# One kernel's table of order rewritten: linear attention followed by a maxout feed-forward layer

## The chip, the cores and the metric

One core of one Trainium2 chip. The metric is the device time of one execution in microseconds (us). The core has five engines that run side by side: TensorE (PE in the profile; its weight loads are shown as PEld), VectorE (DVE), ScalarE (ACT), GpSimd (POOL) and SyncE (SP, which here only issues transfers). Each works through its own list of instructions in order; semaphores make one wait for another. Transfers (DMA) can be issued by SP, ACT and POOL.

## The reference

Eight batches of eight heads, 576 tokens of 64 channels; then 4608 tokens of 512 channels through a layer of 768.

```python
def phi(x):
    proj = np.einsum('bhsd,df->bhsf', x, w_phi)
    proj = proj - np.max(np.abs(proj), axis=-1, keepdims=True)
    return np.concatenate([np.exp(proj), np.exp(-proj)], axis=-1)
q_p, k_p = (phi(q), phi(k))
kv = np.einsum('bhsf,bhsd->bhfd', k_p, v)
z = np.sum(k_p, axis=2)
num = np.einsum('bhsf,bhfd->bhsd', q_p, kv)
den = np.einsum('bhsf,bhf->bhs', q_p, z)[..., None] + 1e-06
x = num / den                      # then to 4608 x 512, heads side by side
h = np.maximum(np.maximum(x @ w1, x @ w2), x @ w3)
out = h @ w_out
```

## The kernel before

**Attention.** The work is cut into 16 units of four heads. A unit loads q, k and v (`L`, `Lv`), brings q and k to bfloat16 (`C`, or in the transfer itself), turns them so that channels lie on partitions (`T` and its copy `Tc` through TensorE in the first four units, a transposing DMA later), projects them (`G`, line 531), takes the largest absolute value of each row (`r`, line 550, DVE), and the two exponentials of the k side (`ek`, line 544, ACT). The q side is projected again with its maximum subtracted (`M`, line 610 or 612/615) and exponentiated (`eq`, line 623, ACT). v is scaled by the exponential of k's maxima (`E`, line 581, ACT; `va`, line 585; `vd`, line 595, the 18-column cast beside it). `K` (line 639) makes the kv sums, `kv` (line 644) copies them out, `N` (line 657) multiplies with the q side, `x` (lines 663 and 664, DVE) divides. `X` turns the result back: through TensorE and a copy `Xc` (line 680) in the first two units, by a transposing DMA (line 687) later.

**Feed-forward.** Nine chunks of 512 tokens, one for each batch and one for the leftover tokens. The maximum of three products is rewritten: w2 and w3 have w1 subtracted (`wd`, line 781), so that h = x w1 + max(0, x(w2-w1), x(w3-w1)), and w1 is folded into w_out once (`wt`, `wm`, `mo`, lines 793 to 811, with `mo` the copy of the folded weight). Each chunk is 12 groups `up`/`up2` of four 128x512 matmuls (line 710), each evacuated by `t1` (line 718 on ACT or 720 on DVE) or `h` (line 716, DVE), then `down` (lines 738 and 743), a copy `osb` (line 751) and a `store` (line 758).

**Order.** The function builds 1471 nodes, numbered as they are made. Each node is one step with its instructions. `PLAN` is a table written out in the file, one word for each node: `51D0@14.7` is node 51, on DVE, buffer slot 0 where the node is the first to use a buffer, with the time 14.7 that a planner gave it. Letters: T is TensorE, D DVE, A ACT, G GpSimd, S SP. The program is issued in the order of the words, so each engine's list is that order restricted to its letter. The times are a planner's due times; on the chip nothing waits for them. They are used in one place: `fill` looks at the gaps between TensorE's due times and puts idlers into them, matmuls on a constant operand whose result nobody reads (line 838), down to gaps of 0.35 us before the due time 28.0 and 0.5 after, and only once the node that clears their operand (node 2) is due to have ended.

```python
n.eng, n.start = {"T": "PE", "D": "DVE", "A": "ACT", "G": "POOL", "S": "SP"}[what[at]], float(start)
n.end = n.start + n.costs[n.eng] + LATENCY[n.eng]
...
gap, t = n.start - free, max(free + 0.1, ready)
while gap > (0.35 if t < WARM else 0.5) and t < n.start - (0.3 if t < 10 else 0.2):
```

**Nodes that the texts name.**

| nodes | what they do |
|---|---|
| 0, 1; 2, 3 | constants: identity and its negative (GpSimd); the idlers' operand and zeros (DVE) |
| 8, 6; 12, 10 | the transfers of the two halves of q and of k of unit 0 (SP) |
| 9, 7; 13, 11 | their casts to bfloat16 (line 448) |
| 84 | the gate: a copy of one row of q (line 460) that holds GpSimd's loads until the first half of q is there |
| 85, 86; 157, 158 | loads of q, k of units 1 and 2 by GpSimd (line 457) |
| 1073, 1074, 1075, 1076 | loads of w1, w2, w3, w_out (line 416) |
| 87, 159 | loads of v of units 1 and 2 |
| 225, 226; 358, 359; 293 | loads of q, k of unit 3; of unit 5; of q of unit 4 |
| 17, 15, 19 | the transposes of unit 0 (line 488) |
| 47, 48, 51, 52; 49, 53 | `va` and `vd` of unit 0; 120, 121, 124, 125 and 122, 126 those of unit 1 |
| 1090, 1092, 1094, 1096 | `mo`, copies of the folded weight (line 811) |
| 81, 83; 154, 156 | `Xc` of units 0 and 1 |
| 229, 231, 233 | `Tc` of unit 3 (line 494) |
| 1099 | the first `up` group |
| 1466, 1470 | the last two stores |

Of the kernel before, what the change touches and what calls it, by code (L numbers as in the profile page):

```python
# [105 lines left out]
66T6@21.4 69T54@21.8 118D@21.8 68A@21.8 67A@22.1 107D@22.1 116A@22.4 163D@22.7 109T60@22.9 71A0@23.1 113D@23.3 100A@23.3  # L106
181T34@23.5 70A@23.8 112D@23.9 123A1@24.1 182A0@24.3 1091T5@24.3 165D@24.5 117D@24.7 119A@24.8 101A@25.0 185D0@25.1
111A@25.4 184D0@25.6 176T61@25.8 127T2@26.1 177A@26.2 179D@26.2 76T7@26.6 183A0@26.7 1092D@26.8 78T3@26.9 120G1@27.0
178A@27.2 136T6@27.2 77D00@27.4 129A1@27.7 133T4@27.7 79D1@28.1 125G@28.1 72T5@28.1 110A@28.1 74T7@28.4 135A@28.6
73D0@28.7 139T0@28.8 126A@29.1 1093T3@29.1 121G@29.2 138A@29.2 75D1@29.3 122A@29.7 140A@29.8 180D@30.0 137A@30.0  # L110
124G@30.3 130T5@30.4 134A@30.5 1094D@30.6 171T71@30.9 141A@31.0 166T64@31.2 128A@31.3 174D@31.4 1075G@31.4 142T30@31.5
172A@31.7 169D@32.0 1078G@32.2 131A@32.2 175D@32.6 186T27@32.6 143A1@32.8 1095T6@32.9 132A@33.1 189D@33.2 170D@33.5
188A@33.6 173A@33.8 145T3@34.1 1079G@34.2 144A@34.3 1096D@34.3 82T2@34.5 149T5@34.7 83A@34.9 146D10@34.9 80T1@35.1
151T0@35.3 168A@35.5 190D@35.6 1089T6@35.7 150D1@35.9 194A0@36.0 187A@36.2 361G1@36.3 81A@36.5 152D0@36.5 147T2@36.9
1090D@37.2 191T3@37.3 228T7@37.4 1077G@37.4 192A0@37.5 167A@37.7 148D1@37.8 193S@37.8 230T5@37.9 229D0@38.4 153T1@38.6
155T0@38.9 231D@39.0 154A@39.1 232T3@39.2 362G@39.5 239T64@39.6 233D@39.6 156A@39.6 249T27@39.8 242D1@40.0 234T51@40.0
# [5 lines left out]
379T24@48.0 367D0@48.2 203A@48.2 198T1@48.3 1121T0@48.5 365A0@48.7 214D@48.8 297G2@49.0 383D0@49.1 202A@49.2 1113T6@49.4
200A@49.6 1122D@49.7 199A@50.1 554S0@50.2 210T7@50.3 382D@50.3 207T5@50.4 1117T0@50.6 211A@50.6 296G@50.6 209A@50.9
1114D@50.9 380A@51.3 266T1@51.5 368D@51.5 1111T2@51.7 298S2@51.8 212A@51.8 381A0@52.1 1118D@52.1 427G0@52.5 1119T6@52.5
267A1@52.6 1112D@52.7 208A@53.0 1115T7@53.4 262A1@53.5 1120D@53.6 268A@53.7 263G1@54.1 265A@54.2 366A@54.3 374T40@54.4
1116D@54.5 369T25@54.6 423S1@54.7 384T61@54.8 371A@55.0 269T3@55.0 372D@55.1 360S0@55.2 1127T7@55.2 385A@55.5 387D@55.6
295S1@55.7 271A@55.7 377D@56.0 216T2@56.1 264G@56.2 553S0@56.2 270A@56.2 222T6@56.4 378D@56.6 370A@56.7 220T4@56.7
275T3@57.0 217D00@57.2 1128T@57.3 375A@57.3 376A@57.8 388D@57.8 373D@58.1 386A@58.2 389T2@58.6 281T01@58.7 221D1@58.7
392A0@58.9 276A@59.1 223D0@59.4 277A@59.5 314T54@59.8 282D1@60.0 272T6@60.1 315A1@60.2 390D0@60.3 1123T3@60.4 426G@60.4
317D1@60.5 391S@60.6 1129A0@60.7 283D@61.1 274A@61.2 278T0@61.2 318D1@61.4 304T25@61.4 557G1@61.5 428S0@61.6 280A@61.6  # L130
309T71@61.6 279A@61.9 1124T@62.0 307D@62.0 316A1@62.2 393G0@62.6 308D@62.6 273A@62.7 312D@63.2 218T0@63.3 305A@63.3
# [738 lines left out]
```

## Time and profile before

| | |
|---|---|
| runs | 291.5, 291.47, 284.21 us; median 291.47 |
| profiled execution | 284.58 us, its span (first to last instruction) 282.8 us |
| busy | TensorE 269.3, DVE 213.0, ACT 190.4, GpSimd 121.9 us |
| idlers | 14 matmuls, 5.6 us busy |
| transfers | HBM read 34.64 MB, written 9.44 MB |

A timeline row reads: start in us, length in us, engine, line of the kernel, operation, output<-inputs, shape, count, and in brackets the idle time of the engine before it with what ended it. A row of a group of instructions has the count, then busy us, mean ns of one, and the idle time before them. A row of waits reads: engine, tile and line, "<-" who released it: us in total, times, longest. A row of windows has for each engine the busy us and the instructions in that stretch, then the granted TensorE clock, the busy share of the DMA engines and GB/s. A group of DMA issues ends with the median us from issue to landing.

### The profile page before, as it was taken

The numbers are of one execution on the slowest core, as the hardware profiler recorded it, in microseconds if no ns is written. First come the engines' busy times: TensorE is split into PE (matmuls) and PEld (weight loads), VectorE is DVE, ScalarE is ACT, GpSimd is POOL, SyncE is SP. The second block draws the span as 40 slices with busy tenths as digits, with TensorE's granted clock in tenths as the row PEclk, the third lists the DMA queues.
The fourth block names the chain that finished last, engine by engine and source line by source line (L and its number), as shares of the span: only waits on it lengthen the run. The fifth ranks groups of instructions, "written<-read, shape, count | busy, mean of one in ns | idle before, by whom it ended". The sixth has DMA issues, their size and how long they took to land.

```text
span 282.8 us, 8452 instructions
## 1 busy us (share of the span) xinstructions
PE 269.3 (95%) x3497; PEld 152.7 (54%) x3536; DVE 213.0 (75%) x444; ACT 190.4 (67%) x445; POOL 121.9 (43%) x103
## 2 busy tenths in 40 slices
PE   3998999999999999999999999999999999999995
PEld 1565675466565555555565556654544555444443
DVE  4899999999889789888898879895683367036432
ACT  2789989997889999776895989758546750211010
POOL 4773999487458232808536755050535000000000
PEclk9999999999999999999999999999999999999999
DMA  6999959999998989996999997888143114500164
GB/s 214 219 211 286 295 91 233 273 313 199 276 216 293 197 166 288 307 234 168 252 246 198 304 199 194 165 172 208 70 93 68 41 41 93 111 2 0 39 139 157
DMA packets 67680, 51.43 MB, mean 182 GB/s; under 512 B 48762, under 2 KB 52922, under 8 KB 67642
## 3 DMA queue, kind: packets, MB, share of 16 engines
q1 hardware_dynamic: 62554, 42.87, 63.5%
q0 software_dynamic: 4576, 7.28, 12.2%
q10 hardware_dynamic: 512, 0.75, 0.7%
q8 instruction: 27, 0.44, 0.6%
q14 instruction: 11, 0.09, 0.1%
HBM read 34.64 MB, written 9.44 MB: 156 GB/s over the span
## 4 chain that ended last, share of the span: by engine, by line
PE 89%; DVE 7%; issue 1%; DMA 1%; ACT 0%; DVEq 0%
PE ups L710 33%; PE ops L743 16%; PE ops L738 10%; PE psn L657 7%; PE kvps L639 6%; PE psq L531 5%; PE psm L610 5%; DVE mqp L550 2%; PE pm L807 1%; DVE mk L550 1%; PE idler L838 1%; DMA q_raw<-in_q_dram 1%; DVE x_sb L664 1%; PE psm L612 1%; DVE w_bf L781 1%
## 5 line engine op out<-in xcount | busy, mean ns | idle before, releaser
L710 PE MATMUL ups<-xT,w_bf 128*128 128x512 bf16 x413 | 101.6, 379 | 1.1
L585 POOL TENSOR_TENSOR vab<-v_raw,em 128x1152 bf16<-128x1152 f32 (+1 forms) x35 | 66.8, 1926 | 60.8 <-ACT em L581 49.7
L544 ACT ACTIVATE Ek<-psk 128x512 bf16<-128x512 f32 (+1 forms) x156 | 82.7, 579 | 13.0 <-PE psk L531 10.0
L623 ACT ACTIVATE Eq<-psm 128x512 bf16<-128x512 f32 (+1 forms) x160 | 82.2, 588 | 12.6 <-PE psm L610 11.9
L710 PEld LDWEIGHTS <-w_bf 128*128 128x128 bf16 x432 | 40.2, 98 | 45.3 <-issue 0.7
L550 DVE TENSOR_REDUCE mqp<-psq 128x4 bf16<-128x512 f32 (+1 forms) x80 | 48.8, 632 | 4.0 <-PE psk L531 3.4
L743 PE MATMUL ops<-wout_bf,hT 128*128 128x512 bf16 (+2 forms) x216 | 50.3, 373 | 0.5 <-issue 0.3
L550 DVE TENSOR_REDUCE mk<-psk 128x4 f32<-128x512 f32 (+1 forms) x78 | 48.4, 635 | 2.8 <-PE psk L531 1.5
L716 DVE TENSOR_TENSOR hT<-hT,ups 128x512 bf16<-128x512 bf16 x54 | 35.8, 681 | 12.8 <-PE ups L710 8.8
L751 ACT COPY osb<-ops 128x512 f32<-128x512 f32 x19 | 11.5, 606 | 34.3 <-PE ops L743 34.0
L664 DVE TENSOR_TENSOR x_sb<-psn,rden 128x320 bf16<-128x320 f32 x64 | 31.5, 492 | 2.4 <-DVE rden L663 0.2
L743 PEld LDWEIGHTS <-hT 128*128 128x128 bf16 x222 | 20.6, 98 | 22.3
L720 DVE TENSOR_SCALAR hT<-ups 128x512 bf16<-128x512 f32 x28 | 18.8, 686 | 17.3 <-PE ups L710 15.0
L657 PEld LDWEIGHTS <-Eq 128*128 128x128 bf16 x640 | 25.4, 97 | 8.3
L657 PE MATMUL psn<-kv_sb,Eq 128*128 128x65 bf16 x640 | 27.2, 194 | 0.1
L531 PE MATMUL psq<-w,qkT 64*128 64x128 bf16 x284 | 23.8, 217 | 0.4 <-DVE qkT L494 0.4
L738 PE MATMUL ops<-xT 128*128 128x512 bf16 x89 | 23.9, 379 | 0.3
L531 PE MATMUL psk<-w,qkT 64*128 64x128 bf16 x284 | 23.9, 217 | 0.0
L718 ACT ACTIVATE hT<-ups 128x512 bf16<-128x512 f32 x26 | 15.8, 616 | 11.8 <-PE ups L710 11.7
L610 PE MATMUL psm<-qkT,wphi_m 128*128 128x512 bf16 (+1 forms) x70 | 22.4, 358 | 0.6 <-DVE hT L720 0.5
L531 PEld LDWEIGHTS <-qkT 64*128 64x128 bf16 x568 | 16.4, 94 | 11.3 <-issue 8.2
L639 PE MATMUL kvps<-vab,Ek 64*128 64x65 bf16 x1152 | 20.5, 190 | 0.6 <-issue 0.6
(79 smaller groups left out, 233.3 us busy)
## 6 DMA issues: line engine op xcount, KB each, us to landing
out_dram<-osb SPq DMA_DIRECT2D x64, 128.0 KB, 2.7
v_raw<-in_v_dram SPq DMA_DIRECT2D x14, 576.0 KB, 6.1
k_raw<-in_k_dram SPq DMA_DIRECT2D x11, 576.0 KB, 4.9
q_raw<-in_q_dram SPq DMA_DIRECT2D x11, 576.0 KB, 5.2
w_bf<-in_moe_w_dram POOLq DMA_DIRECT2D x3, 768.0 KB, 9.0
v_raw<-in_v_dram POOLq DMA_DIRECT2D x2, 576.0 KB, 14.9
qk_bf<-in_q_dram POOLq DMA_DIRECT2D x3, 288.0 KB, 9.5
qk_bf<-in_k_dram POOLq DMA_DIRECT2D x3, 288.0 KB, 11.8
```

The source lines that it names most:

```text
L531: nc.tensor.matmul(ps()[:, i, :], lhsT=cols[r, :], rhs=w2[r, c, :], start=True, stop=True)
L544: nc.scalar.activation(Ek[s]()[:, tiles_of(t0, n), :], of(1), EXP, scale=1.0 - 2.0 * s)
L550: nc.vector.tensor_reduce((mq, mk)[c]()[:, tiles_of(t0, n)], of(c), AXX, ALU.max, apply_absolute_value=True)
L585: (nc.vector if n_.eng == "DVE" else nc.gpsimd).tensor_tensor(vab()[:, g, t0:t1, 0:D], vb()[:, t0:t1, :], em()[:, g, t0:t1].unsqueeze(2).t ...
L610: nc.tensor.matmul(psm()[:, 0:w], lhsT=wphi_m, rhs=rhs, start=True, stop=True)
L623: nc.scalar.activation(Eqb()[s][:, cols], psm()[:, 0:w], EXP, scale=1.0 - 2.0 * s)
L639: nc.tensor.matmul(kvps[ab]()[:, t // NT, g, :], lhsT=Ek[g]()[r, t, :], rhs=vab()[r, g, t, :], start=(t + g == 0), stop=(t == UT - 1 and g ...
L657: nc.tensor.matmul(psn()[:, c, :], lhsT=Eqb()[g][:, t0:t0 + P], rhs=kv()[:, pr, ab, g, :], start=(g == 0), stop=(g == 1))
L710: nc.tensor.matmul(ups(), lhsT=w_bf[i + 1][:, ct, j * P:(j + 1) * P], rhs=tokens_of(ct), start=(ct == 0), stop=(ct == CT - 1))
L716: nc.vector.tensor_tensor(hT()[:, j, :], hT()[:, j, :], ups(), ALU.max)
L738: nc.tensor.matmul(ops_()[:, 0:width], lhsT=tile_of(ct, tt), rhs=line_w[c_i > MOVE][:, ct, cols], start=(ct == 0), stop=False)
L743: nc.tensor.matmul(ops_()[:, 0:width], lhsT=hT()[:, j, tt * P:(tt + 1) * P], rhs=wout_bf[:, j, cols], start=False, stop=(j == JT - 1))
```

## The change

The table `PLAN` is replaced by another one; no other line is touched. It has the same 1471 nodes. 84 nodes stand on another engine (among them 24 `t1`, 14 `osb`, 14 `kv`, 14 `vd`, 6 `mT`, 2 `mo`), the order on every engine differs, and buffer slots (PSUM banks among them) are given out anew. On DVE 352 nodes stand in place of 370, on ACT 443 in place of 430, on GpSimd 107 in place of 98, on SP 110 in place of 114; TensorE keeps its 459. Between TensorE's nodes on 64 rows or 64 columns and the others there are 75 changes in place of 77. The last due time is 275.8 in place of 277.4; by the rules of `fill` the new due times make 20 idlers in place of 14, twelve of them (in place of four) ahead of the first transposes.

The start of both tables:

```diff
-4A@0.7 8S0@0.7 12S0@1.1 10S@1.6 6S@2.0 14S0@2.5 9D0@3.5 84G1@3.5 0G@3.7 2D0@4.1 85G@4.3 3D@4.3 13A@5.0 86G@5.0 5D@5.5
-1G@5.8 17T1@5.8 11D@5.9 1073G@6.3 18D0@6.6 7A@6.8 157G2@7.1 36T23@7.4 15T4@7.7 158G@7.8 38A0@7.8 39D0@7.8 31T56@8.3
-16D@8.4 1076G@8.5 32A0@8.8 34D@9.0 21T71@9.2 33A@9.2 87G1@9.3 26T24@9.4 25D0@9.6 37A@9.7 19T5@9.7 1074G@10.0 27A@10.2
-20D@10.2 24D@10.4 41T5@10.6 28A@10.7 358G1@10.8 29D@11.0 43A@11.1 23A@11.4 225G0@11.5 44D@11.6 30D@11.9 60T7@12.1
-40D@12.5 63T2@12.5 92T4@13.1 45D@13.1 64A0@13.2 88T3@13.3 35D@13.4 22A@13.7 89D1@14.0 46A0@14.1 54T6@14.2 50A@14.3
-42A@14.6 57T1@14.6 51D0@14.7 61A@14.8 94T35@15.2 65A@15.3 97D1@15.6 59A@15.8 226G@15.9 90T2@16.0 98D1@16.2 47G@16.6
-1085T3@16.6 93D@16.8 95A1@16.9 91D@17.0 1087T4@17.2 96A1@17.4 1086D0@17.6 52G@17.7 114T2@17.8 49A@17.9 62A@18.0
-1083T5@18.1 1088D@18.2 55A@18.5 99T37@18.7 1084D@18.8 359G1@18.8 58A@18.9 104T04@19.0 108D@19.4 115A@19.4 53G@19.5
-48G@19.7 160T5@19.9 102D@20.0 106A@20.1 164T1@20.4 56A@20.6 161D2@20.6 162T3@20.7 159G2@20.8 105A@21.1 103D@21.2
...
-124G@30.3 130T5@30.4 134A@30.5 1094D@30.6 171T71@30.9 141A@31.0 166T64@31.2 128A@31.3 174D@31.4 1075G@31.4 142T30@31.5
...
-294S0@43.5 238D@43.8 255A@43.9 293S0@44.0 245A@44.1 253D@44.4 204T4@44.4 1105T1@44.6 1104A@44.6 197G@44.7 1082G@44.9
...
+0G@0.7 2D0@0.7 4A@0.7 8S0@0.7 3D@0.8 12S0@1.1 1G@1.3 10S@1.6 6S@2.0 14S0@2.5 9D0@3.6 84G1@3.6 85G@4.1 5D@4.2 86G@4.8
+13A@5.1 1073G@5.5 11A@5.9 17T1@5.9 158G2@6.3 18D0@6.6 157G@7.0 7A@7.0 31T23@7.3 1076G@7.7 33A0@7.8 34D0@7.8 15T4@7.8
+32A0@8.2 36T56@8.4 16D@8.5 87G1@8.5 19T7@8.8 38A@8.8 20D@9.1 1074G@9.2 21T12@9.2 39D@9.3 26T47@9.5 23A@9.7 29D@9.9
+41T5@10.0 28A@10.1 25D0@10.5 42A@10.6 27A@10.9 44D@11.1 22A@11.4 24D@11.4 88T4@11.7 43A@11.8 30D@12.0 63T2@12.4
+89D1@12.6 60T1@12.8 65A0@13.0 35D@13.2 57T7@13.3 62A@13.5 45D@13.8 92T4@13.8 61A@14.0 40D@14.1 94T35@14.3 46A0@14.5
+90T1@14.7 95A1@14.7 97D1@14.7 47G0@14.8 64A@15.2 93D@15.3 54T3@15.5 98D1@15.5 50A@15.7 59A@15.9 49G@15.9 1085T4@15.9
+48G@16.1 91D@16.1 96A1@16.4 1083T2@16.4 1086D0@16.7 37A@16.8 1087T1@16.9 51G@17.2 53A@17.3 1084D@17.3 58A@17.4
+114T5@17.4 99T04@17.8 55A@17.9 118D@17.9 104T67@18.1 52G@18.3 56A@18.4 108D@18.5 162T2@18.7 103D@19.1 105A@19.2
+160T3@19.2 225G0@19.4 106A@19.7 107D@19.7 359G1@20.1 101A@20.2 102D@20.3 69T76@20.5 116A@20.7 358G1@20.8 161D2@20.9
+100A@20.9 115A@21.4 1088D@21.5 226G@21.5 109T04@21.6 119A1@21.7 71A0@21.9 164T3@21.9 117D@22.1 70A@22.1 66T1@22.3
+159G2@22.3 113D@22.4 1091T6@22.6 67A@22.7 68A@23.0 1075G@23.0 163D@23.0 123A@23.2 110A@23.4 112D@23.6 111A@23.9
+181T75@23.9 176T12@24.2 165D@24.2 183A0@24.4 1092D@24.4 139T0@24.5 121G1@24.5 136T3@24.8 182A0@24.9 179D0@25.0
+127T4@25.3 177A@25.3 185D0@25.6 124G@25.6 72T6@25.7 129A1@25.9 133T1@26.0 184D@26.2 140A@26.4 76T5@26.5 141A@26.6
+126G@26.7 73D00@26.8 120G@26.9 137A@26.9 78T7@27.0 74T0@27.3 134A@27.4 180D@27.4 1093T6@27.6 138A@27.9 125G@28.0
+77D1@28.0 128A@28.3 75D0@28.7 135A@28.8 130T3@28.9 293G0@29.1 178A@29.3 1094D@29.3 171T54@29.4 166T01@29.7 131A@29.8
```

and their ends:

```diff
-1459T2@269.7 1405A3@269.9 1406S@270.6 1456T@270.6 1460T@271.9 1457A0@272.1 1458S@272.7 1463T7@273.2 1461A1@273.4
-1452T@273.8 1462A@274.0 1464T@275.1 1453D2@275.3 1454A@276.1 1467T4@276.1 1465D3@276.3 1468T@276.6 1466A@276.9
-1469D0@277.1 1470S@277.4
...
+1457A1@271.0 1458A@271.6 1452T@272.1 1461D0@272.3 1462S@273.0 1464T@273.4 1453A3@273.6 1454A@274.2 1467T2@274.4
+1465D2@274.6 1468T@274.9 1466A@275.2 1469D1@275.4 1470A@275.8
```

More of the change, by code (lines that the diff above doesn't have):

```diff
@@ L112 @@
[L112 to L116, printed above, removed]
@@ L122 @@
[L122 to L126, printed above, removed]
@@ L127 @@
[L127 to L131, printed above, removed]
@@ new lines @@
+1027D@210.5 983A@211.0 1022D@211.1 1020A@211.5 1348D@211.7 1349T5@211.7 1026A@211.9 1023D@212.3 1359T7@212.6 1028D@212.9
+1341T3@213.4 1042A1@213.6 1360D@213.6 1021A@213.8 1044G1@214.0 993T6@214.3 1039T2@214.4 990T7@214.5 995A@214.6
+1040D1@214.7 1357T1@214.7 992A@214.9 1041S@214.9 1343T2@215.6 1043G@216.0 1332T@216.4 1344D@216.6 1358D@217.2
+1375T2@217.7 1333A2@217.9 1425G@218.1 1342A@218.4 1045G@218.4 996T10@218.7 1350A@218.9 994A@219.3 991A@219.6
+1061T35@219.8 998D0@220.0 997A@220.1 1351T6@221.0 1062A1@221.1 1063D@221.1 1325A1@221.3 984T7@221.8 1326S@221.9
@@ new lines @@
+1071D0@230.3 1064T1@230.6 1376T@230.9 1065D1@231.1 1072S@231.8 1367T3@232.2 1364T@233.1 1368T@234.4 1426G@235.4
+1372T@235.7 1369D1@235.8 1379T7@236.9 1383T6@237.8 1380A0@238.0 1377A3@238.5 1391T0@238.7 1384D@238.9 1378S@239.1
+1435T1@239.5 1392D@239.7 1334S@240.3 1431T3@240.4 1411T7@241.3 1381T2@242.1 1365A3@242.2 1432A1@242.6 1366S@242.8
+1437T6@243.0 1436A@243.1 1403T0@243.8 1370S@244.0 1438A@244.0 1382A@244.5 1397T5@244.7 1389T3@245.6 1395T1@246.4
+1385T6@247.3 1396D@247.5 1399T2@248.2 1386D@248.4 1387T1@249.0 1398D@249.1 1401T6@249.9 1388A@250.1 1390A@250.6
@@ new lines @@
+1400D@250.7 1407T5@250.8 1402D@251.3 1415T1@251.6 1393T3@252.5 1433T2@253.3 1394D@253.5 1373D2@254.1 1463T6@254.2
+1434D@254.7 1445T3@254.9 1374S@254.9 1408T@255.7 1446D@255.9 1427T4@257.0 1409A3@257.2 1447T2@257.9 1428D@258.1
+1443T3@258.7 1448D@258.9 1416T@259.6 1404T@260.9 1417D1@261.1 1449T5@262.2 1405A2@262.4 1406S@263.0 1429T4@263.1
+1439T2@263.9 1430D@264.1 1418S@264.2 1444D@264.7 1459T1@264.8 1440D@265.3 1294S@265.4 1451T0@265.6 1450D@265.9
+1455T4@266.5 1410S@266.6 1441T3@267.4 1412T@268.2 1442D@268.4 1456T@269.5 1413A2@269.7 1414S@270.3 1460T@270.8
```

227 lines of the change are left out of this document (112 added, 115 removed).

## The prediction

> **What bounds the kernel now.** I read the page's first part first, then the windows, then who waits for whom, and last the timeline of the first 42 us.
>
> ```profile
> span 282.8 us, 8452 instructions
> PE 269.3 (95%) x3497; PEld 152.7 (54%) x3536; DVE 213.0 (75%) x444; ACT 190.4 (67%) x445; POOL 121.9 (43%) x103
> ...
> core 0: us, PE busy (x) PEld busy (x) DVE busy (x) ACT busy (x) POOL busy (x), PEclk, DMA share, GB/s
> ...
> 10.00:40.00 30.00, 27.05 (x557) 19.42 (x561) 28.65 (x62) 26.46 (x69) 22.19 (x22) 1.00 1.07 232
> ...
> 40.00:280.00 240.00, 236.92 (x2904) 130.69 (x2935) 179.20 (x367) 160.42 (x372) 93.42 (x68) 1.00 0.74 175
> ```
>
> There are two stages. From 10 to 40 us VectorE (DVE) is busy 28.65 of 30 us, with ScalarE (ACT) close behind at 26.46: there the vector work is the bound. From 40 to 280 us TensorE is busy 236.92 of 240 and DVE only 179.20. What TensorE waits for in that second stage is this list of waits, for the window 40 to 280 and the matmuls alone, complete, and the first row of the same list for the weight loads:
>
> ```profile
> PE psm L610 <- DVE hT L720: 0.5, 1, 0.5
> PE ops L743 <- issue: 0.3, 2, 0.2
> ...
> PEld L531 <- issue: 8.2, 20, 0.4
> ```
>
> The matmuls lose 0.8 us in 240 to waits. So the second stage can hardly be shortened by any order of the same matmuls; what a new order can win must be won before 42 us, and TensorE then carries it to the end.
>
> The start and the end of the first stage, from the timelines of DVE, TensorE and ACT:
>
> ```profile
> 3.73 0.75 DVE L448 CAST qk_bf<-q_raw 128x576 bf16<-128x576 f32 x1 [3.73 <-DMA q_raw<-in_q_dram]
> 4.46 0.17 DVE L409 MEMSET idle<- 128x128 bf16 x1
> ...
> 7.46 0.69 DVE L494 COPY qkT<-tps 128x1024 bf16<-128x1024 bf16 x1 [0.29 <-PE tps L488]
> ...
> 4.68 1.89 PE L838 MATMUL idler<-idle 128*128 128x512 bf16 x4 [4.68 <-DVE idle L409]
> 6.37 1.05 PE L488 MATMUL tps<-ident,qk_bf 128*128 128x128 bf16 x8
> ...
> 8.70 0.62 PE L488 MATMUL tps<-ident,qk_bf 128*128 128x128 bf16 x8
> ...
> 5.64 0.67 ACT L448 CAST qk_bf<-k_raw 128x576 bf16<-128x576 f32 x1 [3.05 <-DMA k_raw<-in_k_dram]
> 7.42 0.67 ACT L448 CAST qk_bf<-q_raw 128x576 bf16<-128x576 f32 x1 [1.10 <-DMA q_raw<-in_q_dram]
> ...
> 40.63 1.18 ACT L680 COPY xT<-pxT 128x576 bf16<-128x576 bf16 x2 [0.77 <-PE pxT L677]
> ...
> 41.89 0.82 PE L710 MATMUL ups<-xT,w_bf 128*128 128x512 bf16 x2
> ```
>
> The idlers, which warm TensorE, start at 4.68 because DVE clears their operand behind a cast that waits for the first landing. The first eight transposes take 1.05 us, the same eight at 8.70 take 0.62: the first group ran at the slow clock.
>
> **The change, part by part.** (a) *Warm-up.* Nodes 2 and 3 go ahead of the first cast, so DVE clears the operand in the 3.7 us in which it waits anyway; by the rules of fill the idlers become 20 instead of 14, twelve of them before the first transposes. The transposes still start at 6.37, since they hang on the ACT cast of 5.64. They run warm: 1.05 - 0.62 = **-0.43 us**, straight on the chain (DVE waits for them at 7.46). Bounds: 0 if the clock is still slow at 6.37, -0.43 if not; I take -0.43.
>
> [...]
>
> (b) *Work taken from DVE.* Up to the first `up` group (node 1099) TensorE's nodes are the same ones in both tables. Before the transposes' copies of unit 3 DVE has four instructions fewer: a cast of k (11), one scaling of v (51) and two copies of the folded weight (1096, 1090).
>
> ```profile
> 10.01 0.68 DVE L550 TENSOR_REDUCE mqp<-psq 128x4 bf16<-128x512 f32 x1
> 10.61 0.68 DVE L550 TENSOR_REDUCE mk<-psk 128x4 f32<-128x512 f32 x1
> ...
> 15.65 0.75 DVE L585 TENSOR_TENSOR vab<-v_raw,em 128x576 bf16<-128x576 f32 x1
> ...
> L811 DVE CAST xT<-pm 128x512 bf16<-128x512 f32 x4 | 2.7, 684 | 0.4 <-PE pm L807 0.4
> ...
> 40.00 1.48 DVE L494 COPY qkT<-tps 128x1024 bf16<-128x1024 bf16 x3
> ```
>
> Two 0.68 us instructions follow each other at 0.60 (10.01, 10.61), so a removed one is worth 0.60 and the scaling about 0.70: 0.70 + 2 x 0.60 = **-1.9 us** of DVE's 28.65. The cast of k lies before 7.46, where DVE waits anyhow: 0.
>
> (c) *Given back at the end of the stage.* Node 156, the second copy of xT of unit 1, goes from ACT to DVE and stands behind the three copies of 1.48 us. Before, DVE's last division ended at about 40.08 and the ACT copies at 40.63 + 1.18 = 41.81, 1.73 later. After, it is about 1.40 for the three copies (0.08 of them overlapped) and 0.68 (the 684 ns of L811) for the copy: 2.08. **+0.3 us.**
>
> (d) *What ACT takes on.* Two folded-weight copies and one 18-column cast come, three 18-column casts go to GpSimd or away:
>
> ```profile
> L751 ACT COPY osb<-ops 128x512 f32<-128x512 f32 x19 | 11.5, 606 | 34.3 <-PE ops L743 34.0
> ...
> L595 ACT CAST vab<-em 128x18 bf16<-128x18 f32 x3 | 0.9, 302 | 0.0
> ```
>
> 2 x 0.606 + 0.302 - 3 x 0.302 = +0.61 us, so 26.46 becomes 27.07 in a stage that (a) to (c) shorten by 2.0 to 28.0. That is 97% busy, and ACT has 3.54 us of idle time in the stage today. Between nothing given back and all 2.0, I take **+0.4 us**: ACT only has to fill idle time that in part waits for DVE.
>
> (e) *GpSimd's queue.* The constants 0 and 1 move ahead of the gate, so the weights and the loads of units 1 and 2 are issued about 0.5 us sooner or a little more, beside the first q and k. Six loads (nodes 225, 359, 358, 226, 159, 1075) then stand in a row, behind five pieces of unit 0's v and ahead of unit 1's v.
>
> ```profile
> 12.35 0.71 POOL L457 DMA_DIRECT2D qk_bf<-in_q_dram  x1 [0.47 <-ACT Ek L544]
> 15.86 0.70 POOL L457 DMA_DIRECT2D qk_bf<-in_k_dram  x1 [2.80 <-DMA w_bf<-in_moe_w_dram]
> ...
> 20.80 0.76 POOL L470 DMA_DIRECT2D v_raw<-in_v_dram  x1
> ...
> 26.06 4.48 POOL L585 TENSOR_TENSOR vab<-v_raw,em 128x576 bf16<-128x576 f32 x4 [4.51 <-ACT em L581]
> ...
> 29.39 1.15 POOL L585 TENSOR_TENSOR vab<-v_raw,em 128x576 bf16<-128x576 f32 x1
> ...
> q_raw<-in_q_dram POOLq DMA_DIRECT2D x1, 576.0 KB, 18.7
> k_raw<-in_k_dram POOLq DMA_DIRECT2D x1, 576.0 KB, 15.3
> ```
>
> Four scalings at 1.15, a cast at 0.3 and six issues at about 0.76 fill 9.5 us from 15.2 (DVE's own scaling starts at 15.65 before, less 0.43): GpSimd is free near 24.7, where unit 1's scale factors are due (26.06 less the gain). The cover of 4.51 us is used up, but not overdrawn: 0. Without it, each microsecond there delays unit 1's K matmuls, and with them everything. Later landings hurt nobody at 15 to 18.7 us: the loads issued near 20 are cast near 36. Node 293, a load of unit 4, comes off SP and lands by 29 + 18.7 = 48, where its cast stands in the table order: 0 to 0.5, taken as 0.
>
> (f) *The later 74 changes of engine* (24 first evacuations, 14 output copies, 14 of kv, ten small casts, six mT, two row copies of mT, three stores, one weight difference): they move net work from DVE to ACT where neither is full (179.20 and 160.42 of 240 us) and where TensorE waits 0.8 us. At most that 0.8 can go; a wait like the 0.5 at L610 can come at any place. 0.
>
> (g) *Alternation.* Groups on 64 rows alternate with full ones 77 times before, 75 after. The weight loads idle 8.2 us at 20 such places, 0.41 each; from the last projection to the first `up` is 0.15 us (the matmul ahead of 41.89 starts at 41.74, the mate of the one quoted below). Two changes fewer: 0 to -0.8, I take **-0.2**.
>
> ```profile
> 41.74 0.22 PE L531 MATMUL psk<-w,qkT 64*128 64x128 bf16 x1
> ...
> 272.07 8.24 SPq L758 DMA_DIRECT2D out_dram<-osb  x6
> ...
> 276.71 3.29 ACTq L758 DMA_DIRECT2D out_dram<-osb  x3
> ...
> 33.87 0.54 PE L639 MATMUL kvps<-vab,Ek 64*128 64x65 bf16 x23 [0.56 <-issue]
> ```
>
> (h) *Tail.* The last store goes from SP, whose last issue ends at 280.31, to ACT, whose previous issue ends at 280.00; one more there, of the 3.29 / 3 = 1.1 us that three take with their waits, or the 0.5 that is the bare issue, comes to 280.5 to 281.1: 0 to +0.8, taken **+0.2**.
>
> Sum: -0.43 - 1.9 + 0.3 + 0.4 - 0.2 + 0.2 = -1.6. The profiled execution took 284.58 us, span 282.8 and 1.78 around it; I predict a span of 281.2 and **283.0 us**. That stands beside the low one of the three runs (284.21); two others took 291.5, so the median of 291.47 holds 6.9 us of which the profiled execution shows nothing.
>
> **Own range of the forecast.** Low: the whole of (b), nothing back in (d) (-0.4 more), -0.8 in (g) (-0.6 more) and the 0.56 us gap at 33.87 gone, in which the K group stood still for no reason that the profile shows: 281.4. High: (d) at +1.4: 284.0.
>
> **Rivals.**
> *ACT takes DVE's place.* If ACT's 3.54 us of idle time stay as they are, 27.07 + 3.54 = 30.6 and the stage is no shorter for (b): (a), (c), (g) and (h) are left, -0.43 + 0.3 - 0.2 + 0.2 = -0.1, and the time is 284.4. For it: 26.46 of 30 busy. Against: its idle time mostly ends with DVE's results, which come sooner.
>
> *The median's extra 6.9 us stay.* Nothing in the profile tells what they are. If they come from outside the order (memory, the clock later on), the middle run is 291.47 - 1.6 = 289.9. If they come from the start (late warm-up, late landings), the change goes at them, and the middle run is 283.0, 2.9% below the old median.
>
> *GpSimd blocks* (the other side). At 15.86 its issue stood 2.80 us until a weight load had landed, with about eight loads unlanded. Six issues in a row can meet the same limit. The first block is no longer hidden by the 4.51 us; three make 8.4 us and 284.58 - 1.6 + 8.4 = 291.4, over 2% slower than the profiled execution; it decides from the third. Against: by 20 us five of the eight earlier loads should be down, so that the queue holds six or seven.
>
> **How the numbers follow.** Forecast 0.53, ACT 0.12, the median's extra staying 0.27, GpSimd 0.06, something else 0.02. A difference of 2% is about what a measurement of this kernel can tell from no change. Against the like run the forecast is -0.6% and counts as the same; against the old median it is -2.9% and counts as faster, if that median repeats: I give that 0.31 of the 0.53, and 0.02 of ACT's 0.12 likewise. Faster 0.33; same 0.22 + 0.10 + 0.27 + 0.01 = 0.60; slower 0.07. The range goes from 281.4 to 290.4, to take in the forecast and the 289.9.
>
> **What would show it.** Idlers from below 1 us and the first eight transposes at about 0.62; the first `up` near 40.3 instead of 41.89; DVE about 1.9 us less up to there and ACT over 95% from 10 to 38; unit 1's v on GpSimd from about 24.7 without a DMA wait; no new wait of TensorE over 1 us after 42. It is wrong if GpSimd waits for a DMA between 19 and 25, if ACT is what DVE then waits for, or if TensorE waits over 2 us later on.

## The result and the profile after

The changed kernel takes **283.12 us** in the median (20 executions, 281.72 to 288.41), 285.16 for the kernel before beside it (20 executions, 283.87 to 293.01). The ratio is 0.994, interval 0.991 to 0.997: no difference of 2%. In a later set on another chip it was 282.85 against 287.27, ratio 0.991 (0.987 to 0.995). The ratios leave out executions more than 1.5% above the fastest of their kernel; four executions of 355 to 710 us, one each of four kernels, are left out of the counts below, though not of the medians over all executions.

The median of before moves with the draw: 291.47 over the three executions shown first, 285.16 over the 20 that hold them, then 287.3, 285.95 and 287.27 in three other sets. Its executions fall into groups, and the experiments below show that these depend on the kernel, since they go with an edit of a word or two:

| executions | up to 286.5 us | 286.5 to 288.5 | over 288.5 |
|---|---|---|---|
| before, four sets | 56 | 22 | 39 |
| after, two sets | 27 | 1 | 0 |

Among the executions up to 286.5 us alone, the change brings the median from 284.47 to 283.09 in the first set (-1.4) and from 284.97 to 282.85 in the later one (-2.1). In the three sets of the experiments the mean granted clock of before's executions goes with the groups: 0.998 or more in every one up to 286.5 us, 0.992 to 0.994 in most of those between 286.5 and 290.6, and 0.981 to 0.988 in those over 291. The profile of the warm start alone, below, has a stretch of 3.41 us at 0.50 of the clock. One such stretch takes 3.41 x 0.5 / 283 = 0.006 off the mean; by this estimate most of the long executions lose what about one to three of them would take.

The profiled execution went from 284.58 to 282.99, its span from 282.8 to 281.1.

The page of the changed kernel, first part, and its windows (us, then busy us and instructions of TensorE, its weight loads, DVE, ACT, GpSimd; granted clock, DMA share, GB/s):

```profile
span 281.1 us, 8518 instructions
PE 273.2 (97%) x3542; PEld 153.6 (55%) x3542; DVE 201.2 (72%) x426; ACT 197.0 (70%) x455; POOL 126.6 (45%) x112
...
10.00:40.00 30.00, 28.24 (x587) 20.25 (x584) 28.53 (x62) 27.32 (x70) 25.40 (x25) 1.00 1.11 250
...
40.00:280.00 240.00, 236.42 (x2896) 129.29 (x2893) 167.60 (x347) 164.69 (x379) 94.06 (x73) 1.00 0.72 174
```

DVE is as full as before from 10 to 40 us, since the stage ends sooner and its successor starts inside the window. Where it ended is in the timelines of TensorE, ACT and GpSimd:

```profile
1.04 5.30 PE L838 MATMUL idler<-idle 128*128 128x512 bf16 x12 [1.04 <-DVE idle L409]
6.14 0.75 PE L488 MATMUL tps<-ident,qk_bf 128*128 128x128 bf16 x8
...
39.44 1.90 PE L710 MATMUL ups<-xT,w_bf 128*128 128x512 bf16 x8
...
4.54 0.67 ACT L448 CAST qk_bf<-k_raw 128x576 bf16<-128x576 f32 x1 [1.92 <-DMA k_raw<-in_k_dram]
...
19.40 0.77 POOL L457 DMA_DIRECT2D qk_bf<-in_q_dram  x1
...
23.04 0.81 POOL L416 DMA_DIRECT2D w_bf<-in_moe_w_dram  x1
23.86 2.29 POOL L585 TENSOR_TENSOR vab<-v_raw,em 128x576 bf16<-128x576 f32 x2
```

The first `up` matmul starts at 39.44 instead of 41.89, 2.45 us sooner. The six issues on GpSimd follow each other from 19.40 to 23.85 without a wait. The last matmul ends only 1.76 us sooner (279.54 to 277.78): 0.7 us is given back on the way, and the list of waits of TensorE's matmuls, 40 to 280 us, complete, points at one place:

```profile
PE kvps L639 <- POOL vab L595: 1.0, 1, 1.0
PE kvps L639 <- POOL vab L585: 0.2, 1, 0.2
```

At 131 us K of a later unit waits 1.0 us for a small cast (node 655, moved from ACT to GpSimd), which stands behind casts on GpSimd that wait for their loads. In a second profile of the changed kernel, taken in the later set, the first `up` starts at 39.73 and this wait is 1.4 us.

### The profile page after: what moved, and what is told of

It reads as the page before. It is cut to its first block, busy times and chain, and to the rows that moved or that the text cites. A ratio compares the mean times of both kernels' runs of the same rounds, so it can differ in the third digit from the quotient of the medians.

```text
span 281.1 us, 8518 instructions
## 1 busy us (share of the span) xinstructions
PE 273.2 (97%) x3542; PEld 153.6 (55%) x3542; DVE 201.2 (72%) x426; ACT 197.0 (70%) x455; POOL 126.6 (45%) x112
## 4 chain that ended last, share of the span: by engine, by line
PE 81%; POOL 7%; DMA 6%; DVE 3%; issue 1%; ACT 1%; POOLq 0%
PE ups L710 30%; PE ops L743 15%; PE ops L738 11%; PE psn L657 6%; PE kvps L639 6%; PE psq L531 4%; PE psm L610 4%; DMA q_raw<-in_q_dram 3%; POOL vab L585 2%; DMA qk_bf<-in_k_dram 2%; POOL w_bf L781 2%; POOL qk_bf L474 2%; DVE mqp L550 1%; PE pm L807 1%; DVE mk L550 1%
## 5 line engine op out<-in xcount | busy, mean ns | idle before, releaser
L585 POOL TENSOR_TENSOR vab<-v_raw,em 128x1152 bf16<-128x1152 f32 (+1 forms) x36 | 68.2, 1908 | 83.9 <-ACT em L581 39.5
L544 ACT ACTIVATE Ek<-psk 128x512 bf16<-128x512 f32 (+1 forms) x156 | 81.5, 575 | 11.9 <-PE psk L531 9.3
L623 ACT ACTIVATE Eq<-psm 128x512 bf16<-128x512 f32 (+1 forms) x160 | 80.4, 584 | 3.5 <-PE psm L610 2.8
L743 PE MATMUL ops<-wout_bf,hT 128*128 128x512 bf16 (+2 forms) x222 | 51.1, 373 | 0.0
L751 ACT COPY osb<-ops 128x512 f32<-128x512 f32 x25 | 14.6, 589 | 33.2 <-PE ops L743 24.1
L718 ACT ACTIVATE hT<-ups 128x512 bf16<-128x512 f32 x32 | 18.8, 616 | 18.2 <-PE ups L710 18.1
L720 DVE TENSOR_SCALAR hT<-ups 128x512 bf16<-128x512 f32 x22 | 15.0, 686 | 12.5 <-PE ups L710 12.5
L531 PE MATMUL psk<-w,qkT 64*128 64x128 bf16 x284 | 23.1, 217 | 0.0
L610 PE MATMUL psm<-qkT,wphi_m 128*128 128x512 bf16 (+1 forms) x70 | 21.8, 358 | 0.0
```

Source lines behind the costliest of these rows:

```text
L531: nc.tensor.matmul(ps()[:, i, :], lhsT=cols[r, :], rhs=w2[r, c, :], start=True, stop=True)
L544: nc.scalar.activation(Ek[s]()[:, tiles_of(t0, n), :], of(1), EXP, scale=1.0 - 2.0 * s)
L585: (nc.vector if n_.eng == "DVE" else nc.gpsimd).tensor_tensor(vab()[:, g, t0:t1, 0:D], vb()[:, t0:t1, :], em()[:, g, t0:t1].unsqueeze(2).t ...
L610: nc.tensor.matmul(psm()[:, 0:w], lhsT=wphi_m, rhs=rhs, start=True, stop=True)
L623: nc.scalar.activation(Eqb()[s][:, cols], psm()[:, 0:w], EXP, scale=1.0 - 2.0 * s)
L743: nc.tensor.matmul(ops_()[:, 0:width], lhsT=hT()[:, j, tt * P:(tt + 1) * P], rhs=wout_bf[:, j, cols], start=False, stop=(j == JT - 1))
```

## The experiments

The kernels stand in three sets, each set on a chip of its own with the kernel before beside it. Only a few words of the table change in each. For small differences I compare the medians of the executions up to 286.5 us with those of before in the same set.

| kernel | executions: up to 286.5, to 288.5, over | median of the first group, and less that of before | ratio and interval |
|---|---|---|---|
| warm start alone | 5, 6, 1 | 285.38, +0.7 | 1.002 (0.998 to 1.007) |
| DVE work put back | 12, 0, 0 | 284.26, -0.4 | 0.996 (0.993 to 0.999) |
| new first stage alone | 9, 0, 0 | 282.94, -1.8 | 0.993 (0.990 to 0.996) |
| node 655 early | 10, 1, 0 | 282.68, -2.0 | 0.989 (0.985 to 0.993) |
| before, 1080 moved | 5, 6, 0 | 283.96, -1.0 | 1.000 (0.995 to 1.006) |
| after, 1080 back | 12, 0, 0 | 284.31, -0.6 | 0.995 (0.991 to 0.998) |
| before, warm, 1080 moved | 11, 0, 0 | 283.10, -1.8 | 0.992 (0.989 to 0.995) |
| after, cold start | 12, 0, 0 | 284.19, -0.7 | 0.994 (0.991 to 0.998) |
| before, 51 moved | 9, 3, 0 | 284.57, -0.4 | 1.000 (0.997 to 1.004) |
| before, 51 and 1080 moved | 11, 0, 1 | 284.47, -0.5 | 0.997 (0.995 to 1.000) |
| after again | 8, 0, 0 | 282.85, -2.1 | 0.991 (0.987 to 0.995) |
| after, two steps moved | 12, 0, 0 | 283.33, -1.6 | 0.993 (0.990 to 0.996) |

### The first set: where the gain is

**The warm start alone**, in the order of before.

```diff
-0G@3.7 2D0@4.1 3D@4.3 1G@5.8
+2D0@0.7 0G@0.7 3D@0.8 1G@1.3
```

> The table of before with one part of the change: nodes 0, 1, 2 and 3 go to the front with the due times of the new table; fill then makes 22 idlers, twelve of them ahead of the first transposes. Theory (step a of the prediction): the first eight transposes take about 0.75 us instead of 1.05, and the profiled execution is 0.3 to 0.43 us shorter than that of before, 284.2 us; the first up group stays at 41.4 or later. Rival, that the early start of the constants and of GpSimd's loads is the heart of the change: at least 1.2 us shorter, 283.4 or less. Second question, whether a cold or reopened clock is behind the long executions of before (287 to 293 us): if so, the five timed runs of this kernel hold none over 286.5; if not, about two of the five do.

Measured: 286.88 us in the median, seven of twelve executions over 286.5. So a warm start alone does not do away with the long ones. The profiled execution is itself one of them, 287.69 us. In its profile (helper lines are numbered one lower in this set) the first `up` starts at 40.00, 1.9 us sooner than in before, and then the gain is lost. Timelines of DVE and GpSimd, the list of waits, and windows of 3.41 us:

```profile
46.09 3.68 DVE L780 TENSOR_TENSOR w_bf<-w_bf 128x1024 bf16<-128x1024 bf16 x1
...
42.85 4.20 POOL L780 TENSOR_TENSOR w_bf<-w_bf 128x1024 bf16<-128x1024 bf16 x2
47.00 1.13 POOL L473 CAST qk_bf<-k_raw 128x1152 bf16<-128x1152 f32 x1
48.08 1.14 POOL L473 CAST qk_bf<-q_raw 128x1152 bf16<-128x1152 f32 x1
...
PE psm L609 <- DVE hT L719: 2.3, 1, 2.3
...
48.28:51.69 3.41, 1.21 (x5) 0.58 (x6) 3.41 (x5) 2.06 (x5) 1.15 (x2) 1.00 0.96 347
51.69:55.10 3.41, 3.41 (x10) 1.32 (x9) 2.70 (x5) 1.82 (x5) 0.94 (x1) 0.50 0.38 148
```

One half of a weight difference, node 1080, takes 3.68 us on DVE, and ends at 49.77, 0.55 us after the second of two casts on GpSimd (48.08 + 1.14 = 49.22). TensorE waits 2.3 us behind it, is busy 1.21 of 3.41 us, and the granted clock of the next 3.41 us is 0.50. The change moves this node to GpSimd.

**The work taken from DVE put back** in the changed kernel.

```diff
-51G@17.2 1096A@33.1 1090A@36.3
+51D@16.15 1096D@33.12 1090D@36.3
```

> The table of after with three instructions put back on VectorE: one scaling of unit 0's v (51) and the copies 1096 and 1090 of the folded weight. Theory (step b): VectorE is the bound up to 39 us, 0.70 + 2 x 0.60 = 1.9 us more on it; what ScalarE and GpSimd then save hides a part; the first up group comes 1.2 to 1.9 us later than the 39.2 of after, and the time is 1.0 to 1.9 us longer, 284.0 to 284.9. Rival, that VectorE had slack by then and the gain came from the earlier start and from GpSimd's order: first up group within 0.5 us of after, time within 0.5 of 283.0.

Measured: 284.26 us, and the first `up` at

```profile
41.23 1.90 PE L709 MATMUL ups<-xT,w_bf 128*128 128x512 bf16 x7
```

instead of 39.44, or 39.73 in the second profile. The three steps are worth 1.5 to 1.8 us there, and 0.9 to 1.7 us in time. Node 51 met GpSimd here too, and these rows of DVE and GpSimd are needed below:

```profile
17.77 1.00 DVE L584 TENSOR_TENSOR vab<-v_raw,em 128x576 bf16<-128x576 f32 x1
...
17.01 2.78 POOL L584 TENSOR_TENSOR vab<-v_raw,em 128x576 bf16<-128x576 f32 x2
```

**The first stage of the changed kernel, then the order of before** (all words due before 46 us from the new table, the rest from the old one; node 1080 is with the rest, on DVE).

> The order of after for everything due before 46.0 in its table, and for the rest the order, engines and slots of before. Theory: the first up group is 2.4 us earlier than before, and the 1.8 us that is left of it at the end shows that the second stage of after gives back 0.7 us, 1.0 of it in one wait of the K group of unit 9 for GpSimd; the order of before has no such wait, so this kernel is 0.4 to 0.7 us shorter than after, 282.4. Rival, that what is given back is the price of being earlier (loads and ScalarE are then late, whatever the order): the same as after, 283.0, with a new wait of TensorE of 0.5 us or more somewhere in 46 to 240.

Measured: 282.94 us: the whole gain is in the first stage, and the old order after it does not do better. The theory's 282.4 was missed; the rival came out, and in its profile TensorE has a new wait of 0.6 us for a transfer at 155 us. Node 1080 shows its own time here, since GpSimd stood still beside it (timelines of DVE and GpSimd):

```profile
46.95 0.68 DVE L780 TENSOR_TENSOR w_bf<-w_bf 128x1024 bf16<-128x1024 bf16 x1
...
42.40 4.21 POOL L780 TENSOR_TENSOR w_bf<-w_bf 128x1024 bf16<-128x1024 bf16 x2
47.78 1.14 POOL L473 CAST qk_bf<-k_raw 128x1152 bf16<-128x1152 f32 x1 [1.17 <-PE psk L530]
```

0.68 us alone, 3.68 beside GpSimd. In before it took 1.88, and GpSimd's rows there tell why:

```profile
44.03 4.19 POOL L781 TENSOR_TENSOR w_bf<-w_bf 128x1024 bf16<-128x1024 bf16 x2
48.17 1.13 POOL L474 CAST qk_bf<-k_raw 128x1152 bf16<-128x1152 f32 x1
49.40 1.46 POOL L474 CAST qk_bf<-q_raw 128x1152 bf16<-128x1152 f32 x1
...
47.98 1.88 DVE L781 TENSOR_TENSOR w_bf<-w_bf 128x1024 bf16<-128x1024 bf16 x1
```

By these lengths it waited through the end of the difference and through the cast of 48.17, and ran in about the last 0.68 us before 49.86; the next cast took 1.46 instead of 1.13. The 0.5 us wait of TensorE that the prediction quoted at L610 ends just behind it, at 50.5 us.

**Node 655 ahead of three casts** on GpSimd in the changed kernel.

```diff
-655G@129.1
+655G@124.85
```

> The table of after with one word moved: node 655, the 18-column cast of unit 9 on GpSimd, is issued ahead of three casts to bfloat16 that wait for loads, not behind them. Theory: the 1.0 us wait of TensorE at 131 us (kvps for vab) goes, nothing else is late there, and the time is 0.8 to 1.1 us shorter than after, 282.0. Rival, that the K group then waits for something else that is as late (its weight loads show a wait of 1.1 us that ended with VectorE): the same as after, 283.0, within 0.3.

Measured: 283.07 us. The wait at 131 us is gone, and another, at 154 us, stands in the list:

```profile
PE psm L609 <- DVE mqp L549: 0.8, 1, 0.8
```

Against before its ratio is 0.989, the changed kernel's 0.991 to 0.994, with overlapping intervals: no gain is shown.

### The second set: node 1080 and the warm start

**Before with node 1080 on GpSimd** (`1080D@46.4` becomes `1080G@46.4`).

> The kernel before with one step moved: node 1080, a half of a weight difference, goes from VectorE to GpSimd at the same place of the order. Theory: on VectorE it waits until GpSimd pauses (1.88 us in the profile of before, 3.68 us in that of the warm start alone, 0.68 us in that of the new order's first stage, where GpSimd stood idle), TensorE starves behind it at 48 us, and where the pause is long enough the granted clock falls. So without it the executions above 287 us go, and the median falls from about 287 to 284.3 us; the shortest ones, 284.2, move by at most 0.7 us. Rival, the long executions come from the cold start or from the order after 50 us: the median stays within 0.5 us of before's and a third of the executions or more stay above 287 us.

Measured: 287.5 us, six of eleven executions from 287.4 to 288.3 us. So node 1080 isn't the whole cause, and the theory in that form falls; five of eleven are at 283.7 to 284.4. But none is over 288.5, where ten of the 35 of before beside it are. The execution that was profiled took 355 us at a granted clock of 0.75, so its times are not compared with others; its order of events points to the other cause. Timelines of DVE and GpSimd, the wait, and the windows:

```profile
16.34 4.02 DVE L585 TENSOR_TENSOR vab<-v_raw,em 128x576 bf16<-128x576 f32 x1
...
16.03 0.70 POOL L457 DMA_DIRECT2D qk_bf<-in_k_dram  x1 [2.79 <-DMA w_bf<-in_moe_w_dram]
16.74 2.27 POOL L585 TENSOR_TENSOR vab<-v_raw,em 128x576 bf16<-128x576 f32 x2
18.95 0.76 POOL L470 DMA_DIRECT2D k_raw<-in_k_dram  x1
19.71 0.76 POOL L595 CAST vab<-em 128x18 bf16<-128x18 f32 x1
...
PE pwT L793 <- DVE mqp L550: 2.4, 1, 2.4
...
19.34:22.75 3.41, 1.60 (x19) 1.29 (x19) 3.41 (x6) 1.17 (x4) 2.89 (x4) 0.75 1.19 276
22.75:26.16 3.41, 3.24 (x49) 2.60 (x49) 3.00 (x6) 2.55 (x7) 0.00 (x0) 0.50 1.14 230
```

The suspect is node 51, the scaling of v on DVE. In the profile of before it ran from 15.65 to 16.40, 0.75 us, and GpSimd's two scalings began behind an issue at 15.86 + 0.70 = 16.56: a margin of 0.16 us. Here DVE was late, GpSimd, which waits for a weight to land, was not; node 51 waited through both scalings and the issue behind them, TensorE lost 2.4 us, and the next window ran at 0.50. No profile of an ordinary execution caught node 51 like this; the third set tests it by moving the node.

**The changed kernel with node 1080 back on DVE** (`1080G@46.6` becomes `1080D@46.6`).

> The changed kernel with that one step back on VectorE, due at 46.6 us as on GpSimd. Theory: GpSimd runs its two differences and then casts from 42 to 49 us without a pause, so VectorE's difference takes 1.9 to 3.7 us instead of 0.7, a stall of 1 to 2.5 us of TensorE comes at 47 to 50 us, and a third or more of the executions run above 285.5 us; median 284.5 us or more. Rival, the one difference is nothing by itself and the new order's slack takes it: median 282.5 to 283.5 us and no more than one execution in ten above 286 us.

Measured: 284.31 us, none over 285.4. Neither: the kernel is 0.8 to 1.5 us longer than the changed one by the executions up to 286.5, but has no long ones. The collision that I expected isn't in its profile; DVE reached the node just in a pause of GpSimd (timelines of DVE and GpSimd):

```profile
47.61 0.68 DVE L781 TENSOR_TENSOR w_bf<-w_bf 128x1024 bf16<-128x1024 bf16 x1
...
48.08 1.21 POOL L474 CAST qk_bf<-k_raw 128x1152 bf16<-128x1152 f32 x1 [0.41 <-DMA k_raw<-in_k_dram]
```

Nor does the profile show where the 0.8 to 1.5 us go. The largest pause of TensorE after 40 us is far from node 1080 and has no releaser:

```profile
64.48 0.64 PE L657 MATMUL psn<-kv_sb,Eq 128*128 128x65 bf16 x15 [1.14 <-issue]
```

Neither profile of the changed kernel has it, and the profile of the cold start below has one of 1.15 us at the same count, the 981st recorded matmul. Its cause stays open, and so does what node 1080 itself costs in this order.

**Before with the warm start and node 1080 moved** (the words of the first and the fifth kernel together).

> The kernel before with two edits: its four setup steps (nodes 2, 3, 0, 1) at the start as in the changed kernel, and node 1080 on GpSimd. Theory: the warm start is worth the 1.9 us that the warm start alone showed at the first up product, and lost them to the VectorE difference: median 282.4 to 283.2 us, as the whole change. Rival, the warm start is worth the 0.43 us of the prediction, and the rest of the 1.9 us is given back at the next wait whatever it is: median 283.8 us or more.

Measured: 283.11 us, no long execution. Two edits reach what the whole table reaches. Beside the kernel with node 1080 moved alone, on the same chip, the warm start takes 0.9 us off the executions up to 286.5 (283.96 to 283.10), and the group at 287.4 to 288.3 is gone. Node 51 is still on DVE, but in the profile it runs from 15.07 to 15.82, while GpSimd's scalings, held by the landing, start at 17.51: the margin is 1.7 us instead of 0.16.

**The changed kernel with a cold start** (the words of the warm start reversed, node 3 at 4.15).

> The changed kernel with the four setup steps back near 4 us, where before has them, so with a cold start. Theory: first up product 1.5 to 1.9 us later, median 284.4 to 284.9 us. Rival by the prediction's own sum: 0.43 us later, median 283.5 us.

Measured: 284.18 us, 0.6 to 1.4 more than the changed kernel by the executions up to 286.5, between both expectations. Its first `up` starts at 39.86, 0.4 or 0.1 later than in the two profiles of the changed kernel: in the new order the first stage hardly hangs on the first transposes. The pause of 1.15 us without a releaser stands in its profile, so the 0.6 to 1.4 us can't be put down to the cold start.

### The third set: both products

**Before with node 51 on GpSimd** (`51D0@14.7` becomes `51G0@15.5`).

> The kernel before with node 51 alone (the v times em product at 15.65 us) on GpSimd, due at 15.5 us, and the cold start and the weight difference on VectorE kept. Theory: in before this 0.75 us product ends 0.16 us before GpSimd's next product begins; in an execution that is a little late it starts beside GpSimd and waits for its next pause, 4.02 us instead of 0.75 as in the profile of the run with node 1080 moved, TensorE stops for 2.4 us at 18.6 us and the granted clock halves for one window of 3.41 us. With the product off VectorE the executions of 289 us and more go; some near 286 to 287.5 us stay, from node 1080. Median near 285.0 us. Rival, the long executions have nothing to do with this product: executions of 289 us and more stay at a fifth of all or more.

Measured: 285.09 us, none over 287.31, where the kernel before beside it had ten of thirty over 289.6. As expected. Node 1080 is still on DVE here, and in the profile it met GpSimd:

```profile
48.38 0.80 DVE L781 TENSOR_TENSOR w_bf<-w_bf 128x1024 bf16<-128x1024 bf16 x1
...
48.59 1.60 POOL L474 CAST qk_bf<-k_raw 128x1152 bf16<-128x1152 f32 x1
```

**Before with nodes 51 and 1080 on GpSimd**, both of the words above.

> The kernel before with both two-input VectorE operations, nodes 51 and 1080, on GpSimd, and the start still cold. Theory: two places where VectorE can be locked out by GpSimd, and no others, make the long executions; with both gone none is over 286.5 us and the median lies at 283.8 to 284.3 us, where before's short executions lie at 284.4 to 286. Rival, the warm start is needed for that as well: a quarter or more stay over 286.5 us.

Measured: 284.52 us; eleven executions from 283.9 to 285.3, and one of 291.7 at a mean clock of 0.95, lower than in any of before's up to 293 us that have a clock on record; its cause stays open, and none over 286.5 was expected. The start is cold, and but for that one the groups are gone. The median is 0.2 us above what I expected.

**The changed kernel again.**

> The changed kernel itself beside the others on the same chip, so that small differences are read within one chip: 282.8 to 283.3 us median, 0.7 to 1.2 us under the order of before with both products moved, if the warm start and the rest of the order are worth that much; the same time, if all the gain is in the two products.

Measured: 282.85 us, 1.7 us under the kernel with both products moved, on the same chip. That is what the new order, its warm start included, is worth beside the two products.

**Two more steps moved** in the changed kernel.

```diff
-655G@129.1  925T2@152.8 916T0@153.0 919T7@153.2 1252T@153.4
+655G@124.85 1252T@152.7 925T2@152.8 916T0@153 919T7@153.2
```

> The changed kernel with two steps moved: the cast for node 655 ahead of three GpSimd casts (the wait of 1.18 us at 131 us goes, as in the run with that edit alone) and the six products of node 1252 ahead of the three of nodes 925, 916 and 919, which at 154 us wait 0.8 us for a transfer. Theory: both waits go and the median is 282.0 to 282.5 us. Rival, as before each removed wait is taken up by the next one: 282.8 to 283.2 us.

Measured: 283.33 us. Both waits are gone, and the whole list for 40 to 280 us is the row below. From the first `up` to the last matmul its profile takes 237.7 us, 238.3 and 238.7 in the two of the changed kernel, but the median is no shorter. The rival holds; no version here is shown to be better than the changed kernel.

```profile
PE kvps L639 <- ACT Ek L544: 0.3, 1, 0.3
```

## Why the prediction was right, and where not

**The sum** said 284.58 - 1.6 = 283.0; the profiled execution took 282.99, the median 283.12. The total is right, but in part by luck. At the first `up` the terms (a) to (d) made -1.6 and 2.45 was measured, chiefly because the 0.7 us of (c) and (d) were not given back there; then 0.7 us was lost in the second stage, where (f) had put nothing.

**(a) Warm-up, -0.43: near the size, but with a step that failed.** In the two profiles of the changed kernel the first eight transposes end at 6.89 and 7.14 instead of 7.42, so 0.53 and 0.28 us sooner. The step that failed is "the transposes still start at 6.37, since they hang on the ACT cast of 5.64". In the profile of before the cast waited for a late landing, ended at 6.31, and held them. In the four other profiles with a cold start the cast starts at 4.68 to 4.75 and the transposes still start at 6.46 to 6.54: there they hang on the four cold idlers in front of them. In the kernel with both products moved the cast starts at 4.75 and the transposes at 6.52; with the warm start and node 1080 moved in before's order they start at 5.40. Timelines of TensorE of these two kernels:

```profile
4.84 1.89 PE L838 MATMUL idler<-idle 128*128 128x512 bf16 x4 [4.84 <-DVE idle L409]
6.52 1.06 PE L488 MATMUL tps<-ident,qk_bf 128*128 128x128 bf16 x8
```

```profile
1.04 4.36 PE L838 MATMUL idler<-idle 128*128 128x512 bf16 x12 [1.04 <-DVE idle L409]
5.40 0.62 PE L488 MATMUL tps<-ident,qk_bf 128*128 128x128 bf16 x8
```

They end at 6.02 instead of 7.58, so 1.6 us sooner, and the first `up` comes 1.8 us sooner (40.53 against 42.30; the two kernels differ in node 51 too). It depends on when the clock opens. The record of the granted clock begins at 8.04 us in the trace of before and at 6.42 in that of the changed kernel, where the transposes start 0.107 us apart up to 6.35 and 0.056 apart from 6.45 on. The twelve idlers start at 1.04 in the five profiles with the warm start that show them, and took 4.36 us with the warm start and node 1080 moved in before's order, 4.45 with two more steps moved, 4.99 with node 1080 back, and 5.30 in both profiles of the changed kernel. In these two it was late (in the second the eight transposes still took 1.01 us), and the transposes began behind the idlers at 6.14 and 6.13. Over executions, the warm start is worth 0.9 us in before's order (the one-word pair on one chip, 283.10 against 283.96). In the new order little of it is shown: with a cold start the first `up` is 0.1 to 0.4 us later, and the rest of the 0.6 to 1.4 us stands beside a pause of unknown cause.

**(b) DVE, -1.9: confirmed**, 1.5 to 1.8 us at the first `up` when the work is put back. What I missed is that node 51 was not only 0.70 us of DVE, but a race with a margin of 0.16 us.

**(c) +0.3 and (d) +0.4 given back: not seen.** The first `up` came at 39.44 and 39.73, not 40.3. Node 156 took 0.45 us, not 0.68, and ACT was busy 25.86 of the 28.40 us from 10 to 38.4, 91% and not over 95: there was room.

```profile
10.00:38.40 28.40, 26.64 (x558) 19.13 (x555) 26.93 (x58) 25.86 (x67) 23.80 (x25) 1.00 1.15 256
...
38.94 0.45 DVE L680 COPY xT<-pxT 128x576 bf16<-128x576 bf16 x1
```

**(e) GpSimd's queue, 0: right in size.** In the first profile there is no wait for a transfer between 19 and 25 us, and unit 1's scalings start at 23.86 (24.7 predicted). In the second the last of the six issues waits 0.52 us for an earlier weight to land, and the scalings start at 25.35. The prediction had named such a wait as a sign of being wrong; the first `up` there is 0.3 us later (39.73), far from the three blocks of 2.8 us of that rival.

```profile
24.07 0.77 POOL L416 DMA_DIRECT2D w_bf<-in_moe_w_dram  x1 [0.52 <-DMA wout_bf<-in_moe_w_out_dram]
```

**(f) The later changes of engine, 0: wrong twice.** Among them was node 1080, "one weight difference", which in the old order goes with a group of long executions (with the warm start, seven of twelve are over 286.5, and none of eleven once the node is moved too); and node 655, at whose cast TensorE waits 1.0 us at 131 us. Both were readable: the 1.88 us of the difference on DVE beside 2.1 on GpSimd, and the move of a cast behind others that wait for loads. The parts don't add up: put back singly, the warm start, the DVE work and node 1080 cost 0.6 to 1.4, 0.9 to 1.7 and 0.8 to 1.5 us, together more than the 1.4 to 2.1 of the whole. The pause of 1.15 and 1.14 us in the profiles of the first and the last of these may be why; nothing in either edit explains it.

**(g), (h)** were not tried apart. The profiles show that the weight loads' waits at line 531 went from 8.2 us at 20 places to 7.3 at 18, and that the span ends 3.3 us behind the last matmul both before (282.8 - 279.54) and after (281.1 - 277.78), so (h) is nearer 0.1 than 0.2; the issue on ACT, for which the prediction has 0.5 us, takes 0.34 to 0.35 there (three issues of line 758 in before). The 0.56 us gap that the low end of the range took away is still there, 0.55 before 31.62.

**The rival of the median's extra 6.9 us** had 0.27. They did not stay: one of 28 executions of the changed kernel is over 286.5. My sentence that the profiled execution "shows nothing" of them was wrong. It showed both places, as a 0.5 us wait at L610 and as a scaling that ended just ahead of GpSimd's. The executions also say what each is worth: with node 51 alone left on DVE (the fifth kernel) the long ones took 287.4 to 288.3 instead of 283.7 to 284.4, with 1080 alone (the ninth) up to 287.3, with both up to 293. In the new order node 1080 on DVE goes with no long executions (none of 12, and none of 9 with the new first stage alone), which fits a step that costs much only where GpSimd runs beside it.

## What to carry to other kernels

A step can be short in the profiled execution because it won a race: node 51 ended 0.16 us ahead of GpSimd's scalings in the profile of before and took 0.75 us. For a step of VectorE like nodes 51 and 1080 (0.75 and 0.68 us alone, up to 4.02 and 3.68 beside GpSimd), look for what GpSimd does beside it and how many tenths of a us lie between them; and where executions of one kernel fall into groups, look for such places before putting them down to the machine. What a warm-up saves is not only in the slow group behind it (here 1.06 to 0.62 us) but also in the queue of idlers in front of that group (its start went from 6.52 to 5.40 us), and it counts only as far as the stage hangs on that group: the first `up` was 1.8 us sooner in before's order, 0.1 to 0.4 in the new one. Before putting a small difference down to an edit, see whether the profile has it at the edit.

## What the runs showed of the hardware

**VectorE behind GpSimd.** The two-operand steps took 0.75 us (node 51, in before) and 0.68 us (node 1080, in the new first stage) alone, and up to 4.02 us (node 1080 moved) and 3.68 us (the warm start alone) beside GpSimd. When they get in differs. Node 51 in the 4.02 us row let two scalings and an issue pass, although it started 0.40 us ahead of the first scaling, in the midst of another issue; node 1080 let two casts pass in the 3.68 us row and one in the 1.88 us row. But in two other profiles, by the lengths of the rows, they got in right behind the instruction that was running, without a pause of GpSimd: node 51 took 1.00 us with the DVE work put back, while GpSimd's two scalings took 2.78 us together instead of 2.27, and node 1080 took 0.80 us with node 51 moved, while GpSimd's next cast took 1.60 instead of 1.14. What decides between these is not shown. In these rows each engine held up the other: VectorE's step waited for GpSimd, in the rows of 4.02, 3.68 and 1.88 us also for scalings or casts begun after it, and where it got in, GpSimd's own rows were longer (2.78 us instead of 2.27, 1.60 instead of 1.14, and 1.46 instead of 1.13 in before). By what means, they do not show.

**The clock.** Stretches in which TensorE was busy 1.21 of 3.41 us (the warm start alone) and 1.60 of 3.41 us (node 1080 moved, in the execution at 0.75) were followed by one of 3.41 us at 0.50 of the clock. In the profile of the new first stage, one with

```profile
276.71:280.12 3.41, 1.71 (x17) 1.13 (x15) 1.54 (x3) 0.00 (x0) 0.00 (x0) 1.00 0.54 196
```

was not: the mean clock over that span of 281.7 us is 1.000. In the two that were, TensorE had waited 2.3 and 2.4 us for VectorE. Where a limit lies, these three rows do not show.
